# Moving side work inside a hand-ordered kernel: attention of two blocks, input parts of two blocks, the last weight pair

## The chip, the cores and the metric

The kernel runs on 1 core of one Trainium2 chip. The metric is device microseconds (us) of one execution, inputs and output in the chip's memory; lower is better. Three runs of the kernel before took 867.34, 867.5 and 868.3 us; their median is 867.5 us. The profile is one execution of its own.

## The reference

Everything is float32. Four batches of 576 positions and 8 heads of size 64 go through a linear attention, and the 2304 rows that come out through two feed-forward layers:

```
kv  = einsum('bhsd,bhse->bhde', k, v)
o   = einsum('bhsd,bhde->bhse', q, kv)
o   = o / sqrt(mean(o*o, axis=-1) + 1e-6) * g_norm     # to x: 2304 x 512
h   = x @ moe_w_in                                     # 512 x 2048
x1  = (h * sigmoid(h)) @ moe_w_out                     # 2048 x 512
out = ((x1 @ moe2_w_a) * (x1 @ moe2_w_b)) @ moe2_w_out # 512 x 1536 twice, 1536 x 512
```

## The kernel before

The 2304 rows are six blocks of 384, numbered 0 to 5. Activations lie transposed: a tile holds 128 features by 384 rows. Each float32 factor of a large product is split in two, a rounded high part (ACT copies it to the type fp32r) and the low rest (DVE subtracts); a product is high times high, low times high and high times low, three matmuls a term. The weights come as raw 128 x 512 pieces that ACT scales (L305, `dec_scale`) and DVE takes apart in three instructions (L311, L317, L324) before the split.

The program has these stretches, in the order of the span:

- 0 to 62 us: attention of blocks 0 and 1 and the first pieces of the first layer, by a list written out.
- 62 to 183 us: steps numbered `g` from 4 to 31. A step multiplies x of one block with one piece of `moe_w_in` (`hp`, L354), passes the result through ACT (sigmoid-weighted, then its high part `gh`, L364) and DVE (low part `gl`, L369), and multiplies the step before with `moe_w_out` (`x1p`, L380). Beside this, steps carry k^T v (`kvps`, L186), attention (`ao`, L220), its norm (`ss` L233, `rr` L238 on POOL, the multiplication L243) and the transposes to x (`xtp`, L256, which ACT copies out as `xf`, L915) of blocks 2 and 3. The `kvps`, `ao` and `xtp` tiles share two buffers of the matmul's output memory.
- to 277 us: eight units, 0 to 7, for blocks 2 and 3 together. A unit has seven products (`X_h`, `Z_h`, `Y_h`, `V_h`, L671) by a scheme with seven multiplications in the place of eight on sums of quarters; after each there is a hook, 0 to 6, into which other work is put. The h values go through DVE (`h`, L827) and ACT (`g`, L837). The sums of x that the scheme needs are the "x parts": pieces T1, hT1, hB11 and so on, in twelve small steps on ACT (L437) and DVE (L438, L487).
- to 335 us: steps on the second half of those units' h values, and beside them attention of blocks 4 and 5. Its q blocks (`qb`, L151) come in by DMA as 8 or 4 small transfers each, DVE transposes them (`qT`, L159), PE multiplies (`ao`).
- to 411 us: units 0 to 7 for blocks 4 and 5, and to 447 us steps again (`x1p`, with `gh_5_n` and `gl_5_n`).
- 447 us to the end: the second layer for blocks 0 and 1, 2 and 3, 4 and 5, from weight sums (`wd`) and x sums (`xcd`) that earlier stretches put into the chip's memory.

The weight sums of the second layer are made in pairs, n from 0 to 11 (`wa0`, `wb0`, `wa1`, ...). A pair is a load (two pieces) and six steps: scale both pieces on ACT; decode the first; decode the second and take the high part; sums (L545 to L548, into two tiles `s_0`, `s_1`); high parts; low parts. Steps hang on hooks of the units; those of the last pair, `wb10` and `wb11`, hang on steps of the stretch after 411 us.

The x sums of blocks 0 and 1 are made by `last_blocks` and `combine` for kt = 0 and kt = 1: `last_blocks` reads x1 of the two blocks back from memory (tiles `b_0_r` and `b_1_r`, four DMAs a kt, L1012), then twelve parts write sums and store them (`xcd`, L439), two small stores a part at most.

What sets the order: the whole program is written out by hand, and each engine works through its own list in order. All DMAs stand in one list, SP's, and are issued in order too: an issue that waits holds back all behind it. `put()` stands in the hooks of units 5 to 7 and releases the stores whose parts have been computed. Tiles are taken from pools. `page` has 37 buffers of 4 KB a partition and `six` has 6 larger ones; a buffer is handed on in the order in which it came free, and the first write into it waits for the last reader of the tile that had it before.

The lines that the change and the prediction touch: `at(g, f)` puts f into step g, `at_unit(b, u, n, f)` into hook n of unit u, `slot(b, h)` counts hooks through the units, seven a unit. `attend`, `turn_q`, `load_q_blocks`, `load_kv`, `kv_pair` are the attention pieces; each takes its step from a tuple of numbers. `prepare(kind, p, roomy)` makes a pair of weight sums; with `roomy` the tile `s_1` comes from `six`, else from `page`.

Of the kernel before, what the change touches and what calls it, by code (L numbers as in the profile page):

```python
# [60 lines left out]
def tile_linattn_moe_moe2(ctx: ExitStack, tc: tile.TileContext, q, k, v, g_norm,  # L61
# [31 lines left out]
    def page(shape, dt, name):  # L93
        return sb.tile(shape, dt, tag="page", bufs=NPAGE, name=name)
# [181 lines left out]
    def load_w(key):  # L276
        kind, f = key
        fs = slice(f * P, (f + 1) * P)
        src = srcs[kind]
        wide = src.dtype != F32  # L280
        if kind in ("wi", "wa", "wb"):
            src = src[:, fs]
        else:
            src = src[fs, :]
        if wide:
            src = src.bitcast(U32)
        if kind in ("wi", "wa", "wb"):
            src = src.rearrange("(kt p) f -> p kt f", p=P)
        r = page([P] + list(src.shape[1:]), U32 if wide else F32, f"raw_{kind}{f}")
        nc.sync.dma_start(r, src)  # L290
        raws[key] = r.rearrange("p k f -> p (k f)") if kind in ("wi", "wa", "wb") else r
# [4 lines left out]
    def dec_scale(key):  # L296
        r = raws[key]
        if r.dtype == F32:
            mids[key] = r
            return  # L300
        r = r.rearrange("p (n t) -> p n t", t=2)
        early = key[0] in ("wi", "wo") and key[1] < 4
        early = early or key[0] == "wb" and key[1] >= NF2 - 2
        m = (page if early else small)([P, DM], U32, f"m_{key[0]}{key[1]}")
        nc.scalar.mul(m.bitcast(F32), r[:, :, 1].bitcast(F32), 2.0 ** -112)  # L305
        mids[key] = m

    def dec_shift(key):
        m = mids[key]
        if m.dtype == U32:  # L310
            nc.vector.tensor_scalar(m, m, 3, None, op0=ALU.logical_shift_left)  # L311
# [15 lines left out]
    def dec_join(key):  # L327
        dec_low(key)
        dec_sign(key)
# [105 lines left out]
    def halve(hi, lo, src, *stores):  # L435

        return (lambda: nc.scalar.copy(hi, src),  # L437
                lambda: nc.vector.tensor_sub(lo, src, hi.bitcast(F32)),  # L438
                *[lambda to=to, t=t: nc.sync.dma_start(to, t.bitcast(F32)) for to, t in stores])  # L439
# [57 lines left out]
    def prepare(kind, p, roomy=False):  # L497


        keys = [(kind, 2 * p + f) for f in range(2)]  # L500
        mat = ("wa", "wb").index(kind)
        H2 = 2 * P
        m, s, wait = [], [], []

        def load():
            for key in keys:
                load_w(key)

        def decode(f):
            dec_shift(keys[f])  # L510
            dec_join(keys[f])
            m.append(mids.pop(keys[f]))

        def flat(t):
            return t.rearrange("p i f -> p (i f)")

        def hi(o, lo, src, to):
            first_, *rest = halve(o, lo, src, to)
            first_()
            wait.append(rest)  # L520

        def rest():
            sub, *put_ = wait.pop(0)
            sub()
            fresh_.extend(put_)

        def scale():
            dec_scale(keys[0])
            dec_scale(keys[1])

        def first_half():
            decode(0)

        def second_half():
            o = page([P, 2, DM], F32R, f"a_{kind}{p}")
            hi(o[:, 0], o[:, 1], m[0], (wd[p, (0, 4)[mat]], flat(o)))
            decode(1)

        def add():
            rest()  # L540
            for h in range(2):
                s.append((six if roomy and h else page)([P, 2, DM], F32R, f"s_{h}_{kind}{p}"))
            a11, a12, a21, a22 = (e[:, h * H2:(h + 1) * H2] for e in m for h in range(2))
            s1, s2, s3, s4 = (s[h][:, 1, i * H2:(i + 1) * H2].bitcast(F32) for h in range(2) for i in range(2))
            nc.vector.tensor_add(s1, a21, a22)  # L545
            nc.vector.tensor_sub(s3, a11, a21)
            nc.vector.tensor_sub(s2, s1, a11)
            nc.vector.tensor_sub(s4, a12, s2)  # L548

        def high():  # L550
            a21, a22 = m[1][:, 0:H2].bitcast(F32R), m[1][:, H2:]
            for h in range(2):
                o = s[h]
                hi(o[:, 0], o[:, 1], o[:, 1].bitcast(F32), (wd[p, ((1, 2), (5, 6))[mat][h]], flat(o)))
            hi(a21, a22.bitcast(F32R), a22, (wd[p, 3, :, mat * DM:(mat + 1) * DM], m[1].bitcast(F32R)))

        def low():
            for _ in range(3):
                rest()

        return load, [scale, first_half, second_half, add, high, low]
# [324 lines left out]
    base = []  # L886
    n = 0
# [5 lines left out]
    def at(g, fn, *args):  # L893
        side.setdefault(g, []).append(lambda: fn(*args))
# [27 lines left out]
    def at_unit(b, u, n, fn, *args):  # L922
        inner.setdefault((b, u, n), []).append(lambda: fn(*args))

    for b, g0s in ((2, (12, 14, 16, 18)), (3, (20, 22, 24, 26))):
        at(g0s[0] - 4, load_kvt, b)
        for g0, p in zip(g0s, (0, 2, 1, 3)):
            at(g0 - 3, load_kv, b, p)
            at(g0, kv_pair, b, p)
    for (j, p), g0 in zip([(2, 0), (2, 2), (3, 0), (3, 2), (2, 1), (2, 3), (3, 1), (3, 3)],  # L930
                          (12, 14, 16, 18, 20, 22, 24, 25)):
        at(g0 - 5, load_q_blocks, j, p)
        at(g0 - 2, turn_q, j, p)
        at(g0, attend, j, p)
        at(-(g0 + 1), norm_mul, j, p)
        at(g0 + 3, stage_f, j, p)
# [52 lines left out]
    def slot(b, h):  # L989
        return (b,) + divmod(min(h, 7 * NF1 // 2 - 1), 7)  # L990

    for n in range(2 * NPAIR):
        load, steps = prepare(("wa", "wb")[n % 2], n // 2, n <= 7)
        if n == 2 * NPAIR - 1:
            at_unit(4, 7, 3, load)
            for i, f in enumerate(steps):
                at(base[8] + 1 + i, f)
            continue
        b, h0 = (2, 7 * (n + 2)) if n < 3 else (4, 7 * (n - 3))
        if h0 == 0:  # L1000
            at(P2A + 14, load)
        else:
            at_unit(*slot(b, h0 - 5), load)
        for f, h in zip(steps, (0, 1, 2, 5, 5, 7)):
            at_unit(*slot(b, h0 + h), f)

    def last_blocks(d, kt):

        t = [page([P, 2, TB], F32, f"b_{kt}_{r}") for r in range(2)]
        for r in range(2):  # L1010
            for n in range(2):
                nc.sync.dma_start(t[r][:, n], x1d[2 * d + n, :, 2 * r + kt, :])  # L1012
        return lambda n, r: t[r][:, n]
# [6 lines left out]
    for kt in range(2):  # L1020
        todo = []

        def blocks0(kt=kt, todo=todo):
            todo.extend(combine(0, kt, half_page, last_blocks(0, kt)))

        def parts0(n, todo=todo):
            for f in todo[n]:
                f()

        at_unit(2, 5 + kt, 6, blocks0)  # L1030
        for n in range(12):
            at_unit(2, 6 + kt, 1 + n // 2, parts0, n)

    made = {}

# [175 lines left out]
    with tc.manual_schedule():  # L1211
# [64 lines left out]
        for n, (d, p) in enumerate(seq):  # L1276
            new = 0 < n < NPAIR
            m = n % NPAIR
            if 1 <= m <= 4 and n < 2 * NPAIR:

                kt, h = divmod(m - 1, 2)
# [53 lines left out]
```

## Time and profile before

| | |
|---|---|
| median of three runs | 867.5 us (867.34 to 868.3) |
| the profiled execution | 866.76 us, of which the span of the trace is 865.0 us |
| PE (TensorE matmul) busy | 850.8 us, 98% of the span, 4966 instructions |
| DVE (VectorE) busy | 622.2 us, 72% |
| ACT (ScalarE) busy | 347.8 us, 40% |
| POOL (GpSimd) busy | 52.6 us, 6% |
| DMA | 230 MB, all queues; 229.15 MB on SP's queue in 127904 packets |
| granted TensorE clock | the highest tenth in all 40 slices |

PE is busy in all but some 14 us, so the time is PE's work and its waits. The chain that ended last runs 83% on PE. Numbers in names are tile numbers of the program: `qb_5_3` is the q block of block 5 for the fourth pair of heads (pairs are numbered 0 to 3), `gl_5_2` the low part of step 2 of the stretch after unit 7. In the trace the numbers are left out.

### The profile page before, as it was taken

The page shows a single profiled execution, that of the slowest core. Times are in us where ns is not written, and L with a number is a line of the kernel's source. Part 1 is how long each engine was busy: PE and PEld are TensorE (multiplying, and loading weights), DVE is VectorE, ACT ScalarE, POOL GpSimd, SP SyncE. Part 2 cuts the span into 40 slices and gives each one's busy share as a digit, 9 for nine tenths or more (in the row PEclk, how much of TensorE's full clock was granted, in tenths as well). Part 3 has the DMA queues.
Part 4 walks back from the last instruction along what each step waited for, and adds up shares of the span by engine and source line. Part 5 has one row for each costly group of instructions (what it writes and reads, how often), then busy time and mean ns, then how long its engine had stood idle before and what let it go on. Part 6 is the DMA issues. An engine that isn't in the chain of part 4 may idle for free.

```text
span 865.0 us, 13734 instructions
## 1 busy us (share of the span) xinstructions
PE 850.8 (98%) x4966; PEld 807.4 (93%) x4967; DVE 622.2 (72%) x1191; ACT 347.8 (40%) x708; POOL 52.6 (6%) x73
## 2 busy tenths in 40 slices
PE   7999999999999999999999999999999999999998
PEld 5799999999998999999999999999999999999996
DVE  4879989777956779989746788876576665545555
ACT  4666765544545456556522533221412211221110
POOL 5430111100000500000000000000000000000000
PEclk9999999999999999999999999999999999999999
DMA  9985886189986659999999998496688475755001
GB/s 276 372 222 160 258 244 234 66 312 405 408 315 183 190 218 336 405 404 385 369 405 417 388 336 333 152 379 242 238 305 276 135 292 200 292 219 195 1 0 74
DMA packets 127972, 230.03 MB, mean 266 GB/s; under 512 B 41504, under 2 KB 87072, under 8 KB 127904
## 3 DMA queue, kind: packets, MB, share of 16 engines
q1 hardware_dynamic: 127904, 229.15, 73.7%
q8 instruction: 39, 0.64, 0.3%
q14 instruction: 29, 0.24, 0.1%
HBM read 160.17 MB, written 68.94 MB: 265 GB/s over the span
## 4 chain that ended last, share of the span: by engine, by line
PE 83%; DMA 9%; DVE 4%; ACT 2%; issue 1%; SPq 1%; POOL 0%; DVEq 0%; ACTq 0%
PE x1p L380 18%; PE op L865 17%; PE hp L354 8%; PE Z_b L671 4%; PE X_b L671 4%; PE V_b L671 4%; PE Z_a L671 4%; PE X_a L671 4%; PE V_a L671 4%; DMA wd<-a_wa 2%; PE V_h L671 2%; PE X_h L671 2%; PE Y_b L671 2%; PE Y_a L671 2%; PE Z_h L671 2%; PE ao L220 2%
## 5 line engine op out<-in xcount | busy, mean ns | idle before, releaser
L380 PE MATMUL x1p<-gh,wo 128*128 128x384 f32 x768 | 195.0, 337 | 0.3 <-ACT gh L364 0.3
L380 PEld LDWEIGHTS x1p<-gh,wo 128*128 128x128 f32 x768 | 138.0, 188 | 0.6 <-ACT gh L364 0.6
L380 PE MATMUL x1p<-gl,wo 128*128 128x384 f32 x384 | 127.9, 337 | 1.1 <-DVE gl L369 1.1
L865 PE MATMUL op<-wp,ab 128*128 128x512 f32 x360 | 83.4, 390 | 0.0
L728 ACT CAST ab<-a 128x384 fp32r<-128x384 f32 x72 | 37.0, 514 | 115.0 <-DVE a L722 58.3
L865 PEld LDWEIGHTS op<-wp,ab 128*128 128x128 f32 x360 | 67.4, 188 | 13.7
L369 DVE TENSOR_TENSOR gl<-g,gh 128x384 fp32r<-128x384 f32 x96 | 54.0, 563 | 30.6 <-ACT gh L364 30.4
L380 PEld LDWEIGHTS x1p<-gl,wo 128*128 128x128 f32 x384 | 71.9, 188 | 2.0 <-DVE gl L369 2.0
L873 DVE TENSOR_TENSOR o<-op,o 128x512 f32<-128x512 f32 x90 | 60.4, 686 | 16.6 <-PE op L865 16.6
L865 PE MATMUL op<-w,ab 128*128 128x512 f32 x288 | 66.9, 390 | 0.0
L865 PEld LDWEIGHTS op<-w,ab 128*128 128x128 f32 x288 | 53.9, 188 | 10.9
L364 ACT CAST gh<-g 128x384 fp32r<-128x384 f32 x96 | 49.2, 513 | 22.4 <-PE x1p L380 20.6
L354 PE MATMUL hp<-xh,wi 128*128 128x384 f32 x256 | 52.7, 345 | 0.4 <-ACT xh L260 0.3
L238 POOL TENSOR_TENSOR rr<-ss,nhalf 128x6 f32<-128x6 f32 x24 | 34.4, 1435 | 229.4 <-DVE ss L233 229.3
L354 PEld LDWEIGHTS hp<-xh,wi 128*128 128x128 f32 x256 | 43.8, 188 | 1.4 <-ACT xh L260 1.0
L671 PE MATMUL X_a<-xc,wp 128*128 128x384 f32 x216 | 43.8, 337 | 0.0
L671 PE MATMUL Z_a<-xc,wp 128*128 128x384 f32 x216 | 43.4, 335 | 0.1
L671 PE MATMUL V_a<-xc,wp 128*128 128x384 f32 x216 | 43.3, 335 | 0.0
L671 PE MATMUL Z_b<-xc,wp 128*128 128x384 f32 x216 | 43.3, 335 | 0.0
L671 PE MATMUL V_b<-xc,wp 128*128 128x384 f32 x216 | 43.3, 335 | 0.0
L671 PE MATMUL X_b<-xc,wp 128*128 128x384 f32 x216 | 43.3, 334 | 0.0
L732 DVE TENSOR_TENSOR ab<-a,ab 128x384 fp32r<-128x384 f32 x72 | 39.8, 553 | 2.2 <-ACT ab L728 0.6
(172 smaller groups left out, 1551.6 us busy)
## 6 DMA issues: line engine op xcount, KB each, us to landing
wp<-wd SPq DMA_DIRECT2D x114, 512.0 KB, 6.5
hw<-hsd SPq DMA_DIRECT2D x32, 512.0 KB, 8.5
xc<-xcd SPq DMA_DIRECT2D x21, 768.0 KB, 8.5
hw<-had SPq DMA_DIRECT2D x16, 768.0 KB, 8.4
raw_wi<-in_moe_w_in_dram SPq DMA_DIRECT2D x16, 512.0 KB, 7.0
raw_wo<-in_moe_w_out_dram SPq DMA_DIRECT2D x16, 512.0 KB, 6.0
hsd<-hs SPq DMA_DIRECT2D x16, 512.0 KB, 5.0
raw_wa<-in_moe_w_a_dram SPq DMA_DIRECT2D x12, 512.0 KB, 7.8
```

Source lines behind the costliest of these rows:

```text
L220: nc.tensor.matmul(o[a:e, i], t[:, i * P + a:i * P + e], kvc[bb, p], start=True, stop=True)
L238: nc.gpsimd.tensor_tensor(r, rms[j, p], nhalf, op=ALU.pow)
L354: nc.tensor.matmul(o, w[wp][:, kt * P:(kt + 1) * P], x[key][:, kt, :], start=(n == 0), stop=(n == 3 * KD - 1))
L364: nc.scalar.copy(gh, src)
L369: nc.vector.tensor_sub(gl, src, gh.bitcast(F32))
L380: nc.tensor.matmul(acc[vi][c], w[wp][:, c * P:(c + 1) * P], gg[vi, s][g], start=(s == s0 and i == 0), stop=(s == s1 - 1 and i == 2))
L671: nc.tensor.matmul(b[bank], w(name, wq, kt), x(i, xq, kt), start=(fresh and k == 0), stop=(k == 5), skip_group_check=True)
L728: nc.scalar.copy(o[:, 0], t)
L732: low = lambda t=t, o=o: nc.vector.tensor_sub(o[:, 1], t, o[:, 0].bitcast(F32))
L865: nc.tensor.matmul(o, ab[d, p, f, n][:, g, ts], wp[p, 7 + f][:, wq * DM:(wq + 1) * DM], start=(k == 0), stop=(k == 5))
L873: nc.vector.tensor_add(t, o, t)
```

## The change

Three edits.

1. k^T v of blocks 2 and 3 moves from steps 12, 14, 16, 18 and 20, 22, 24, 26 to 11, 13, 15, 17 and 19, 21, 23, 25; attention from 12, 14, 16, 18, 20, 22, 24, 25 to 11, 13, ... 25. Loads, q transposes, norms and `xtp` hang on these numbers and move along.
2. Of blocks 0 and 1, kt = 1: the four loads move from hook 6 of unit 6 to hook 3 of unit 6, and the twelve parts from hooks 1 to 6 of unit 7 to hooks 0 to 5. kt = 0 stays where it was.
3. The last pair of weight sums is loaded in hook 2 of unit 7 instead of hook 3, its six steps start in the first step of the stretch after 411 us instead of the second; and `prepare` is given room in `six` for pairs 0 to 6 instead of 0 to 7, so that `s_1_wb3` comes from `page`.

```diff
--- before.py
+++ after.py
@@ -922,13 +922,13 @@
     def at_unit(b, u, n, fn, *args):
         inner.setdefault((b, u, n), []).append(lambda: fn(*args))
 
-    for b, g0s in ((2, (12, 14, 16, 18)), (3, (20, 22, 24, 26))):
+    for b, g0s in ((2, (11, 13, 15, 17)), (3, (19, 21, 23, 25))):
         at(g0s[0] - 4, load_kvt, b)
         for g0, p in zip(g0s, (0, 2, 1, 3)):
             at(g0 - 3, load_kv, b, p)
             at(g0, kv_pair, b, p)
     for (j, p), g0 in zip([(2, 0), (2, 2), (3, 0), (3, 2), (2, 1), (2, 3), (3, 1), (3, 3)],
-                          (12, 14, 16, 18, 20, 22, 24, 25)):
+                          range(11, 27, 2)):
         at(g0 - 5, load_q_blocks, j, p)
         at(g0 - 2, turn_q, j, p)
         at(g0, attend, j, p)
@@ -990,11 +990,11 @@
         return (b,) + divmod(min(h, 7 * NF1 // 2 - 1), 7)
 
     for n in range(2 * NPAIR):
-        load, steps = prepare(("wa", "wb")[n % 2], n // 2, n <= 7)
+        load, steps = prepare(("wa", "wb")[n % 2], n // 2, n <= 6)
         if n == 2 * NPAIR - 1:
-            at_unit(4, 7, 3, load)
+            at_unit(4, 7, 2, load)
             for i, f in enumerate(steps):
-                at(base[8] + 1 + i, f)
+                at(base[8] + i, f)
             continue
         b, h0 = (2, 7 * (n + 2)) if n < 3 else (4, 7 * (n - 3))
         if h0 == 0:
@@ -1027,9 +1027,10 @@
             for f in todo[n]:
                 f()
 
-        at_unit(2, 5 + kt, 6, blocks0)
+        h0 = 43 + 6 * kt
+        at_unit(*slot(2, h0 - 2 - 2 * kt), blocks0)
         for n in range(12):
-            at_unit(2, 6 + kt, 1 + n // 2, parts0, n)
+            at_unit(*slot(2, h0 + n // 2), parts0, n)
 
     made = {}
```

SP's list, in units 6 and 7: `b_0_*` and `b_1_*` are the loads of x1 for kt = 0 and kt = 1, `xcd` the stores of x sums, first where the loads now stand.

```order
 L439 DMA xcd_71<-hB11_0_0_3070 128x384
 L439 DMA xcd_71<-b_0_0_3045 128x384
+L1012 DMA b_1_0_3118<-x1d_68 128x384 x2
+L1012 DMA b_1_1_3119<-x1d_68 128x384 x2
 L439 DMA xcd_71<-hT1_0_0_3073 128x384
 L439 DMA xcd_71<-hB11_0_0_3070 128x384
```

The second piece follows in the same list, six rows further on, where the loads stood; `qb_4_0` and those behind it are q blocks.

```order
 L439 DMA xcd_71<-hT2_0_0_3115 128x384
 L439 DMA xcd_71<-T2_0_0_3101 128x384
-L439 DMA xcd_71<-hB21_0_0_3163 128x384
+L439 DMA xcd_71<-hB21_0_0_3169 128x384
 L439 DMA xcd_71<-b_0_1_3046 128x384
-L1012 DMA b_1_0_3184<-x1d_68 128x384 x2
-L1012 DMA b_1_1_3185<-x1d_68 128x384 x2
-L439 DMA xcd_71<-hB21_0_0_3163 128x384
+L439 DMA xcd_71<-hB21_0_0_3169 128x384
 L439 DMA xcd_71<-hT2_0_0_3115 128x384
-L151 DMA qb_4_0_3209<-in_q_dram 32x6x32 x8
-L151 DMA qb_5_0_3218<-in_q_dram 32x12x32 x4
```

The four loads of `b_1_0` and `b_1_1` are moved ahead of ten stores; the first q load stood two stores behind them and now stands twelve behind. Rows taken out and put in with another number alone (`hB21_0_0`) are the same work; the q loads come again further down in their old order, with the stores of kt = 1 spread otherwise among them: before `qb_5_3`, the last q load, there were 44 q issues and 12 stores from `qb_4_0` on, and there are 44 and 14 now.

PE's list in step 25 (block 3, head pair 3), before:

```order
L380 MATMUL x1p_3_3_1736<-gh_3_12_1907,wo_12_1612 128x384 x2
L380 MATMUL x1p_3_3_1736<-gl_3_12_1912,wo_12_1612 128x384
L256 MATMUL xtp_2_3_1990<-ident_63,sq0_66 128x128 x3
L220 MATMUL ao_3_3_1995<-kvc_0_3_79,qT_3_3_1888 128x128 x3
L354 MATMUL hp_3_14_2009<-xh_1_531,wi_14_1803 128x384 x8
L354 MATMUL hp_3_14_2009<-xl_1_532,wi_14_1803 128x384 x4
```

And now:

```order
L380 MATMUL x1p_3_3_1745<-gh_3_12_1930,wo_12_1625 128x384 x2
L380 MATMUL x1p_3_3_1745<-gl_3_12_1935,wo_12_1625 128x384
L186 MATMUL kvps_3_3_1995<-kv_3_3_1836 64x64 x8
L186 MATMUL kvps_3_3_1995<-kvt_3_1384 64x64 x2
L220 MATMUL ao_3_3_2008<-kvc_0_3_79,qT_3_3_1911 128x128 x3
L354 MATMUL hp_3_14_2022<-xh_1_531,wi_14_1829 128x384 x8
L354 MATMUL hp_3_14_2022<-xl_1_532,wi_14_1829 128x384 x4
```

`ao_3_3` followed directly on `xtp_2_3`; now `xtp_2_3` stands a step ahead, and `kvps_3_3` has come between the step's `x1p` and `ao_3_3`.

DVE's list in the first steps after 411 us (`gl` is the low part that the next `x1p` needs; `m_wb10` and `m_wb11` are the last pair's pieces), before:

```order
L369 TENSOR_TENSOR gl_5_1_4988<-g1_4_0_3965,gh_5_1_4986 128x384
L369 TENSOR_TENSOR gl_5_2_5016<-g1_4_0_3965,gh_5_2_5014 128x384
L311 TENSOR_SCALAR m_wb10_5006<-m_wb10_5006 128x512
L317 SCALAR_TENSOR_TENSOR m_wb10_5006<-raw_wb10_4878,m_wb10_5006 128x512
L324 SCALAR_TENSOR_TENSOR m_wb10_5006<-raw_wb10_4878,m_wb10_5006 128x512
L369 TENSOR_TENSOR gl_5_3_5043<-g1_4_0_3965,gh_5_3_5041 128x384
L311 TENSOR_SCALAR m_wb11_5008<-m_wb11_5008 128x512
L317 SCALAR_TENSOR_TENSOR m_wb11_5008<-raw_wb11_4880,m_wb11_5008 128x512
L324 SCALAR_TENSOR_TENSOR m_wb11_5008<-raw_wb11_4880,m_wb11_5008 128x512
L369 TENSOR_TENSOR gl_5_4_5068<-g1_4_1_4226,gh_5_4_5066 128x384
```

And now:

```order
L369 TENSOR_TENSOR gl_5_1_4992<-g1_4_0_3965,gh_5_1_4990 128x384
L311 TENSOR_SCALAR m_wb10_4980<-m_wb10_4980 128x512
L317 SCALAR_TENSOR_TENSOR m_wb10_4980<-raw_wb10_4868,m_wb10_4980 128x512
L324 SCALAR_TENSOR_TENSOR m_wb10_4980<-raw_wb10_4868,m_wb10_4980 128x512
L369 TENSOR_TENSOR gl_5_2_5019<-g1_4_0_3965,gh_5_2_5017 128x384
L311 TENSOR_SCALAR m_wb11_4982<-m_wb11_4982 128x512
L317 SCALAR_TENSOR_TENSOR m_wb11_4982<-raw_wb11_4870,m_wb11_4982 128x512
L324 SCALAR_TENSOR_TENSOR m_wb11_4982<-raw_wb11_4870,m_wb11_4982 128x512
L369 TENSOR_TENSOR gl_5_3_5048<-g1_4_0_3965,gh_5_3_5046 128x384
L438 TENSOR_TENSOR a_wb5_5033<-m_wb10_4980,a_wb5_5033 128x512
```

The decoding of each piece stands one `gl` sooner; on ACT the scaling of both pieces stood behind `gh_5_1` and now stands ahead of it.

## Rows read from the trace of the kernel before

**Rows 1.** The page: busy time of each engine, its share, and instructions.

```profile
PE 850.8 (98%) x4966; PEld 807.4 (93%) x4967; DVE 622.2 (72%) x1191; ACT 347.8 (40%) x708; POOL 52.6 (6%) x73
```

**Rows 2.** Timeline of PE (start, duration, engine, line, tile, [idle before <-releaser]): five waits.

```profile
155.74 0.94 PE L220 MATMUL ao<-kvc,qT 128*128 128x128 f32 x6 [0.67 <-ACT xf L915]
...
272.49 1.34 PE L671 MATMUL Z_h<-hB_h,hw 128*128 128x384 f32 x6 [0.23 <-DVE h L827]
...
277.40 0.44 PE L380 MATMUL x1p<-gl,wo 128*128 128x384 f32 x1 [1.15 <-DVE gl L369]
...
395.13 1.31 PE L671 MATMUL V_h<-hT_h,hw 128*128 128x384 f32 x6 [0.70 <-DVE u_h L681]
...
425.86 0.62 PE L380 MATMUL x1p<-gh,wo 128*128 128x384 f32 x2 [0.26 <-ACT gh L364]
```

**Rows 3.** Timeline of the DMA queue SP from 256 to 298 us: issues.

```profile
256.33 0.32 SPq L439 DMA_DIRECT2D xcd<-b  x1
...
256.74 0.38 SPq L439 DMA_DIRECT2D xcd<-hT  x1
...
263.46 0.38 SPq L439 DMA_DIRECT2D xcd<-b  x1
...
263.93 1.87 SPq L1012 DMA_DIRECT2D b<-x1d  x4
...
266.84 12.21 SPq L151 DMA_DIRECT2D qb<-in_q_dram  x24
...
296.05 2.01 SPq L151 DMA_DIRECT2D qb<-in_q_dram  x4
```

**Rows 4.** Timeline of PE: unit 6's Z, unit 7's Y, an xtp of block 5.

```profile
260.45 1.21 PE L671 MATMUL Z_h<-hB_h,hw 128*128 128x384 f32 x6
...
262.54 1.21 PE L671 MATMUL Y_h<-hT_h,hw 128*128 128x384 f32 x6
...
301.64 0.49 PE L256 MATMUL xtp<-ident,sq 128*128 128x128 f32 x3
```

**Rows 5.** Timeline of DVE from 269 to 301 us.

```profile
269.81 0.56 DVE L487 TENSOR_TENSOR b<-b,b 128x384 f32<-128x384 f32 x1 [1.02 <-DMA b<-x1d]
...
276.80 0.55 DVE L369 TENSOR_TENSOR gl<-g,gh 128x384 fp32r<-128x384 f32 x1
...
300.04 0.58 DVE L159 STREAM_TRANSPOSE qT<-qb 128x384 f32<-128x384 f32 x1 [0.68 <-DMA qb<-in_q_dram]
...
300.54 0.52 DVE L243 TENSOR_TENSOR sq<-ao,rr 128x384 f32<-128x384 f32 x1
```

**Rows 6.** Timeline of DVE and PE from 90 to 94 us.

```profile
90.04 0.55 DVE L369 TENSOR_TENSOR gl<-g,gh 128x384 fp32r<-128x384 f32 x1
...
93.46 0.57 DVE L159 STREAM_TRANSPOSE qT<-qb 128x384 f32<-128x384 f32 x1
...
91.49 0.34 PE L380 MATMUL x1p<-gl,wo 128*128 128x384 f32 x1
```

**Rows 7.** Timeline of ACT from 415 to 425 us.

```profile
415.62 0.52 ACT L364 CAST gh<-g 128x384 fp32r<-128x384 f32 x1
...
416.03 1.23 ACT L305 ACTIVATE m_wb<-raw_wb 128x512 f32<-128x512 f32 x2
...
424.75 0.66 ACT L584 ACTIVATE m_w<-raw_w 128x512 f32<-128x512 f32 x1 [2.87 <-DMA raw_w<-in_moe_w_out_dram]
```

**Rows 8.** Timeline of DVE and PE from 417 to 420 us.

```profile
418.17 0.42 DVE L311 TENSOR_SCALAR m_wb<-m_wb 128x512 uint32<-128x512 uint32 x1
...
419.95 0.55 DVE L369 TENSOR_TENSOR gl<-g,gh 128x384 fp32r<-128x384 f32 x1
...
417.47 0.34 PE L380 MATMUL x1p<-gl,wo 128*128 128x384 f32 x1
```

**Rows 9.** Timeline of DVE: decoding of the w_a pair before 390 us.

```profile
387.19 0.43 DVE L545 TENSOR_TENSOR s_wa<-m_wa 128x256 f32<-128x256 f32 x1 [0.79 <-DMA wd<-a_wb]
...
388.66 0.43 DVE L546 TENSOR_TENSOR s_wa<-m_wa,m_wa 128x256 f32<-128x256 f32 x1 [1.05 <-DMA wd<-s_wb]
```

## The prediction

> **What bounds the kernel now.** I read the page first. PE is busy 850.8 us, 98% of the span [rows 1], so no engine has to be made faster. The change adds and removes no instruction of PE, DVE, ACT or POOL, and can only take away waits of PE or make new ones. Then I looked through PE's timeline for idle time in the stretches that the edits touch. Five waits lie there [rows 2]: 0.67 us before an `ao` at 155.74 (the `ao` of block 3, pair 3, whose output buffer was that of an `xtp` that ACT had still to copy), 0.23 and 1.15 us in unit 7 (`Z_h` at 272.49, `x1p` at 277.40, both held by DVE), 0.70 us at 395.13, 0.26 us at 425.86. Their sum, 3.01 us, is all that the edits could win there. Third came the issues of SP, the DMA queue, around unit 7 [rows 3], and DVE beside them [rows 5]: here the reader is to see that SP issues one small DMA after another without a pause, and that the last q transpose already waits for it.
>
> **Edit 1, attention.** `ao_3_3` no longer follows directly on `xtp_2_3`, a step of matmuls lies between them, so the copy by ACT (xf) is long done: minus 0.67 [rows 2]. The other `kvps`, `ao` and `xtp` stand to each other as before, a step earlier. What is late next is DVE, which has no free time in steps 10 to 13: a q transpose (0.57 us busy [rows 6]) and a norm's sum come ahead of `gl` where they came behind it. The `gl` at 90.04 ended at 90.59 and its matmul came at 91.49 [rows 6], a slack of 0.90; the two inserted instructions cost half a us each, 1.0 together, and the step's matmuls themselves come a little earlier by what k^T v weighs there. I take plus 0.2 for this step and the one before. The bounds are minus 0.67 with no new wait, and plus 0.5 if such a wait comes in two steps. Edit 1: minus 0.5. The loads that move with it still land more than a step before their use; that cover gone, a wait on one q block would cost the 0.5 us that a late issue costs.
>
> **Edit 2, the x parts.** What it can win is clear: in unit 7 DVE stands 1.02 us for the kt = 1 load at 269.81, and the `gl` at 276.80, which ends at 277.35, starts behind the parts that this held up [rows 5]; PE's 0.23 and 1.15 go, 1.38 us, when the parts come a hook sooner.
>
> What it costs stands on SP. The loads now precede ten stores, and they cannot be issued at once, because their tiles take over buffers still in use: `b_1_0` that of `hw_2_6_2`, which the last matmul of unit 6's `Z_h` reads, and `b_1_1` that of `hT2_h2_0`, which unit 7's `Y_h` reads up to its fifth of six matmuls (the pools' order of release gives both). In the trace these end at 260.45 + 1.21 = 261.66 and at about 262.54 + 0.9 = 263.4 [rows 4]; all of it comes 0.5 earlier by edit 1, so 262.9 for the second. Before, SP used just this time for the ten stores: 256.74 to 263.46 [rows 3]. Now it waits, in order, with the stores behind.
>
> Step by step: the last two loads take 2 x 0.47 (four took 1.87 [rows 3]), up to 263.85. Twelve stores follow, at the pitch of the queue: 24 q issues took 12.21 us, 0.51 each [rows 3], so 12 x 0.51 = 6.1, up to 269.95. There the q loads begin; before they began at 266.84 [rows 3], so they are 3.1 late. From there to the first issue of `qb_5_3` at 296.05 there were 29.2 us for 56 issues, no slack to catch up, and there are now 58. At 0.51 to 0.52 each that ends at 299.6 to 300.2, 3.6 to 4.1 late. I take 3.7.
>
> The transpose of `qb_5_3` waited 0.68 for its DMA, at 300.04 [rows 5], so it has no slack, and comes at 303.74. Next in DVE's list is the norm's multiplication (300.54 [rows 5]), on which PE's `xtp` at 301.64 depends [rows 4]: it ended at 301.06, 0.5 before PE came to it with everything else done. So `xtp` starts at 301.64 + 3.7 - 0.5 = 304.84. This is a point in time, not a delay to be added to others: PE would arrive there at 301.64 - 0.5 - 1.38 = 299.76 and waits, in one piece or with the q blocks before it sharing it. The gains of edits 1 and 2 vanish in it. Balance at 301.64: plus 3.2. The bounds: minus 1.9 if SP is not late, plus 4.5 if each issue behind the loads takes the 0.52 us and `b_1_1` is issued a little later still.
>
> The trace says of issuing that it is slow: 0.51 us each, 24 on end [rows 3]. The Trainium skill (DMA: Bandwidth & Descriptors, section Issuing engines are not separate DMA queues) says that the time to initiate a DMA is usually small beside the DMA itself. By that rule 12 stores ahead of the q loads would cost next to nothing and edit 2 would win its 1.38. The measured pitch decides against it for such small transfers; what it would give is the first rival below.
>
> **Edit 3, the last weight pair.** On ACT the two scalings (1.23 us as a group, some 1.1 up to the next start, since instructions overlap a little [rows 7]) now come ahead of `gh_5_1`, which started at 415.62: it ends at 417.25 and `gl_5_1` at 417.85. PE's first matmul with `gl_5_1` stood at 417.47 [rows 8], so PE waits 0.4. Then each decoding, 418.17 to 419.95 = 1.78 us of DVE [rows 8], stands ahead of a `gl` whose step is only four groups of 0.52 = 2.08 us long. Followed through with these durations, the next four steps wait 0.15, 0.2, 0.45 and 0.3 more: 1.5. Before, the stretch lost 0.26 at 425.86 and the `gl` behind it, some 0.7 in all, because ACT stood 2.87 for a DMA at 424.75 [rows 2, 7]; that wait is now inside the others. Edit 3 net: plus 0.7, bounds 0 and plus 1.3.
>
> `s_1_wb3` from the other pool shifts every later `page` buffer by one. The next pair's `s_0_wa4` then waits for the store of `s_0_wb3`, a later one than before; already now DVE waits 0.79 and 1.05 for such stores [rows 9], and `V_h` at 395.13 is 0.70 late [rows 2] by DVE. This may get worse or better by that 0.7; I take plus 0.1.
>
> **Sum.** Plus 3.2 at 301.64, plus 0.7, plus 0.1: 4.0 us. Against the profiled execution, 866.76 us, that is 870.8. The median of the runs, 867.5, lies 0.74 above it, so a timed run should give 871.5.
>
> **The rivals.**
>
> *SP catches up.* The loads find their buffers free earlier than I read it, or the stores are issued faster than 0.51. Then minus 0.67 and minus 1.38 stand, with edit 3 between 0 and 0.8: 865.4 to 866.3. For it: the pitch in the middle of stores has been 0.47, and b loads and stores need no new data. Against it: 56 issues in 29.2 us leave nothing to give back. It decides when the q loads start before 267.5. 12 in 100.
>
> *The q loads are half as late.* With 2 us of lateness `xtp` is at 303.1, plus 1.5 at 301.64, and with the rest of edit 3 low the sum is 0 to plus 2.3: 867.5 to 869.8. It would come if some stores wait no longer behind the loads, or q blocks land quicker than the 2 us that they took. 22 in 100, half of it within the measurement.
>
> *Only PE's list counts.* Lateness is hidden since DVE's list leaves other work to PE; edits 1 and 3 nearly cancel, and 1.38 is lost again elsewhere: no change, 866.5 to 868. The wait of 0.68 already there [rows 5] speaks against it. 10 in 100.
>
> *It is worse.* The same lateness, and DVE in steps 10 to 13 or at 395 loses another 2 us: 873.5. 6 in 100.
>
> **How the numbers follow.** My forecast, 871.5 with an own range of 870 to 873, has 50 in 100. What can be told from no change for this kernel is about 0.2%, 1.7 us: slower means above 869.2, faster below 865.8. Slower: 50 + 6 + 11 of the half-late case = 67. Within: 11 of the half-late case, 10 of no change and 2 of the first rival = 23. Faster: the first rival's other 10. The range that holds 8 in 10 goes from 866.3, which leaves the first rival out, to 873.2.
>
> **What the new profile would show.** Right: SP's list pauses before the b loads at 261 to 263, q loads start near 270, the last q transpose of block 5 waits some 3 us for its DMA, and PE has a wait of 1 to 4 us before an `xtp` near 300 to 305, while the waits at 155.74 and 277.40 are gone. After 415 us, PE shows small waits on `gl` in four or five steps on end. Wrong: if the q loads start by 267, or PE runs from 285 to 307 without a wait on `xtp`, the main step has failed; if the first `gl` after 415 us is in time, that of edit 3.

## The result, and the profile after

The changed kernel took 871.73 us, the median of 6 runs (870.72 to 873.57), against 867.8 us of before in 6 runs: ratio 1.0052, 95% interval 1.0034 to 1.0069. It is slower by 3.9 us between the medians, by 4.5 going by the ratio. The profiled execution is one of the slower of these, 873.32 us with a span of 871.5; before it was 866.76. What the two traces show is therefore 6.6 us of difference, not 3.9; the part that only some runs have is the last point of this section.

PE's instructions are the same in number, and their busy time rose all the same, from 850.8 [rows 1] to:

```profile
PE 854.4 (98%) x4966; PEld 808.7 (93%) x4967; DVE 620.7 (71%) x1191; ACT 348.1 (40%) x708; POOL 52.7 (6%) x73
```

Of PE's timeline the waits between 150 and 435 us, which answer to [rows 2]:

```profile
257.23 1.32 PE L671 MATMUL V_h<-hT_h,hw 128*128 128x384 f32 x6 [0.65 <-DVE u_h L681]
...
269.41 1.32 PE L671 MATMUL V_h<-hT_h,hw 128*128 128x384 f32 x6 [0.42 <-DVE u_h L681]
...
284.43 0.55 PE L256 MATMUL xtp<-ident,sq 128*128 128x128 f32 x3 [0.52 <-DVE sq L243]
...
291.40 0.55 PE L256 MATMUL xtp<-ident,sq 128*128 128x128 f32 x3 [0.20 <-DVE sq L243]
...
299.41 0.55 PE L256 MATMUL xtp<-ident,sq 128*128 128x128 f32 x3 [1.24 <-DVE sq L243]
...
305.74 0.90 PE L256 MATMUL xtp<-ident,sq 128*128 128x128 f32 x3 [2.65 <-DVE sq L243]
...
389.54 1.34 PE L671 MATMUL V_h<-hT_h,hw 128*128 128x384 f32 x6 [0.98 <-DVE u_h L681]
...
431.14 0.44 PE L380 MATMUL x1p<-gl,wo 128*128 128x384 f32 x1 [0.18 <-DVE gl L369]
```

Of the five waits of before none is left at its place; a `V_h` one unit ahead of that of 395.13 waits 0.98, at 389.54, and a `gl` at 431.14 0.18. New are four waits for an `xtp`, 0.52 + 0.20 + 1.24 + 2.65 = 4.6 us, all released by DVE's norm multiplication. The last one stood at 301.64 [rows 4] and stands at 305.74.

SP's list from 256 to 303 us, which answers to [rows 3] (four loads of x1, then stores, then the q loads):

```profile
256.74 0.32 SPq L439 DMA_DIRECT2D xcd<-b  x1
261.72 2.71 SPq L1012 DMA_DIRECT2D b<-x1d  x4
264.52 0.38 SPq L439 DMA_DIRECT2D xcd<-hT  x1
...
270.53 0.41 SPq L439 DMA_DIRECT2D xcd<-hT  x1
271.00 5.93 SPq L151 DMA_DIRECT2D qb<-in_q_dram  x12
...
277.96 12.93 SPq L151 DMA_DIRECT2D qb<-in_q_dram  x24
...
292.91 3.87 SPq L151 DMA_DIRECT2D qb<-in_q_dram  x8
296.88 0.39 SPq L439 DMA_DIRECT2D xcd<-T  x1
...
300.84 2.01 SPq L151 DMA_DIRECT2D qb<-in_q_dram  x4
```

The reader is to see the hole between 257.06 and 261.72, and then no hole any more: what SP did not do in it comes behind it. The waits of SP in this stretch name the cause, the two matmul groups that still read the buffers (columns: us in total, times, longest):

```profile
SPq L1012 <- PE Z_h L671: 4.6, 1, 4.6
...
SPq L1012 <- PE Y_h L671: 0.8, 1, 0.8
```

The q loads begin at 271.00 (before 266.84), the last begins at 300.84 (before 296.05). DVE's q transposes, which answer to the third of [rows 5], now wait for nearly every q block; the four of those waits that stand ahead of the four `xtp` waits, and the multiplication behind the last:

```profile
283.35 0.58 DVE L159 STREAM_TRANSPOSE qT<-qb 128x384 f32<-128x384 f32 x1 [2.66 <-DMA qb<-in_q_dram]
...
290.32 0.58 DVE L159 STREAM_TRANSPOSE qT<-qb 128x384 f32<-128x384 f32 x1 [2.32 <-DMA qb<-in_q_dram]
...
298.34 0.58 DVE L159 STREAM_TRANSPOSE qT<-qb 128x384 f32<-128x384 f32 x1 [3.36 <-DMA qb<-in_q_dram]
...
304.66 0.58 DVE L159 STREAM_TRANSPOSE qT<-qb 128x384 f32<-128x384 f32 x1 [2.96 <-DMA qb<-in_q_dram]
305.16 0.52 DVE L243 TENSOR_TENSOR sq<-ao,rr 128x384 f32<-128x384 f32 x1
```

The last point is PE's clock. The windows of the changed kernel around the last wait (columns: PE, PEld, DVE, ACT, POOL busy with instructions, granted clock, DMA share, GB/s):

```profile
302.00:305.00 3.00, 1.09 (x7) 0.77 (x5) 0.34 (x1) 1.39 (x4) 0.00 (x0) 1.00 0.79 222
305.00:307.00 2.00, 1.26 (x6) 1.27 (x7) 2.00 (x5) 0.32 (x1) 0.78 (x1) 0.63 0.96 249
307.00:309.00 2.00, 2.00 (x10) 2.00 (x9) 1.51 (x4) 1.25 (x4) 0.85 (x2) 0.52 1.01 378
309.00:311.00 2.00, 2.00 (x14) 1.97 (x13) 2.00 (x6) 0.43 (x2) 1.56 (x1) 1.00 1.01 405
```

PE was idle for 2.65 of the 3 us before 305.74, and then got a clock of 0.63 and 0.52 of full speed in two windows, where the kernel before has 1.00; full speed is the level of 2.4 GHz, a half that of 1.2 GHz. Some 3.4 us at half speed, by the clock of these windows, cost this execution 1.5 to 1.7 us (the same matmuls start 4.1 us behind those of before at 305.74 and 5.6 to 5.8 us behind some 10 us later). Of the six runs four have a mean clock of 0.997 or 0.998 and took 871.2 to 873.57; the two with 1.000 took 870.72 and 870.77. Of the 60 runs of the kernel before beside the experiments one has a mean clock as low as 0.998.

### The profile page after: what moved, and what is told of

Read it like the earlier page. It is cut to its first block, busy times and chain, and to the rows that moved or that the text cites. A ratio compares the mean times of both kernels' runs of the same rounds, so it can differ in the third digit from the quotient of the medians.

```text
span 871.5 us, 13730 instructions
## 1 busy us (share of the span) xinstructions
PE 854.4 (98%) x4966; PEld 808.7 (93%) x4967; DVE 620.7 (71%) x1191; ACT 348.1 (40%) x708; POOL 52.7 (6%) x73
## 4 chain that ended last, share of the span: by engine, by line
PE 80%; DMA 8%; DVE 6%; SPq 3%; issue 2%; ACT 1%; POOL 0%; DVEq 0%; ACTq 0%
PE x1p L380 16%; PE op L865 16%; PE hp L354 8%; PE X_b L671 4%; PE Z_a L671 4%; PE V_b L671 4%; PE X_a L671 4%; PE Z_b L671 4%; PE V_a L671 4%; DMA wd<-s_wa 4%; PE V_h L671 2%; PE X_h L671 2%; PE Z_h L671 2%; SPq L151 2%; PE Y_b L671 2%; PE Y_a L671 2%
```

## The experiments

The theory: SP's list is what costs. The moved loads wait on SP for buffers in use, the twelve stores behind them are put off, and so are the q loads, up to the last, on which PE waits by way of DVE. The rival: the time goes elsewhere, by the parts a hook sooner, by edit 1 or by edit 3. Each kernel ran with kernels of before on the same chip; ratios are to before, and a time against before is the ratio's. A time against the changed kernel is taken from the medians, 871.73 us there; by the ratios it comes out up to 0.4 us larger.

**Each edit alone.** Edit 1 (steps 11, 13, ... in place of 12, 14, ...):

```diff
-    for b, g0s in ((2, (12, 14, 16, 18)), (3, (20, 22, 24, 26))):
+    for b, g0s in ((2, (11, 13, 15, 17)), (3, (19, 21, 23, 25))):
-                          (12, 14, 16, 18, 20, 22, 24, 25)):
+                          range(11, 27, 2)):
```

> The kernel before with edit 1 alone. My theory (the changed kernel loses its time on SP's list, by edit 2): the 0.67 us wait before ao goes, and the trace of the changed kernel stood 1.0 us ahead of before at 190 us; so 0.5 to 1.0 us faster than before, ratio 0.9988 to 0.9994, and the waits at 272 and 277 us stay. Rival (the new places of attention load DVE or SP in the steps and cost later): 1 us or more slower than before.

Measured: 865.99 us, ratio 0.9989 (0.9980 to 0.9998), faster by 0.95. No wait of PE is left at 155. In unit 7 the wait at 277 is still there, and in place of 0.23 before `Z_h` there is one of 0.55 before `V_h`:

```profile
268.80 1.33 PE L671 MATMUL V_h<-hT_h,hw 128*128 128x384 f32 x6 [0.55 <-DVE u_h L681]
...
276.82 0.44 PE L380 MATMUL x1p<-gl,wo 128*128 128x384 f32 x1 [1.12 <-DVE gl L369]
```

So the theory's first term holds and the rival falls. Matmul for matmul, PE gains 0.75 us on the kernel before between 30 and 170 us of this trace.

Edit 2 (loads three hooks sooner, parts one hook sooner):

```diff
-        at_unit(2, 5 + kt, 6, blocks0)
+        h0 = 43 + 6 * kt
+        at_unit(*slot(2, h0 - 2 - 2 * kt), blocks0)
-            at_unit(2, 6 + kt, 1 + n // 2, parts0, n)
+            at_unit(*slot(2, h0 + n // 2), parts0, n)
```

> The kernel before with edit 2 alone. My theory: SP stands still for some 4 us ahead of the kt = 1 loads, the q loads start near 271 us, xtp waits some 4 us in all between 284 and 307; 3 to 5 us slower than before, with a dip of PE's granted clock between 300 and 310 us. Rival (the three edits cost only together, or edit 3 costs most): within 1.5 us of before.

Measured: 873.3 us, ratio 1.0063 (1.0050 to 1.0076), slower by 5.5; a little more than the theory's 5, and far from the rival's 1.5. Its trace has the same waits as the changed kernel:

```profile
298.64 0.55 PE L256 MATMUL xtp<-ident,sq 128*128 128x128 f32 x3 [1.28 <-DVE sq L243]
...
305.08 0.86 PE L256 MATMUL xtp<-ident,sq 128*128 128x128 f32 x3 [2.75 <-DVE sq L243]
```

and four of its five runs show a mean clock of 0.998 or less. The last `xtp` stands at 305.08 without edit 1 and at 305.74 in the changed kernel with it, so what edit 1 wins is lost in this wait.

Edit 3 (last pair a step sooner, one tile from the other pool):

```diff
-        load, steps = prepare(("wa", "wb")[n % 2], n // 2, n <= 7)
+        load, steps = prepare(("wa", "wb")[n % 2], n // 2, n <= 6)
-            at_unit(4, 7, 3, load)
+            at_unit(4, 7, 2, load)
-                at(base[8] + 1 + i, f)
+                at(base[8] + i, f)
```

> The kernel before with edit 3 alone. My theory: small waits on gl after 415 us and a shift of the V_h wait at 395; 0.3 to 1.3 us slower than before, ratio 1.0003 to 1.0015. Rival (edit 3 carries a good part of the loss): over 2 us slower. Second rival (edit 3 costs nothing): within 0.3 us.

Measured: 867.54 us, ratio 1.0003 (0.9994 to 1.0012): plus 0.3 us, not to be told from nothing nor from the lower part of what was expected. Over 2 us is out. The `V_h` wait has shifted as expected (0.65 at 384.82, before 0.70 at 395.13 [rows 2]), and of the waits on `gl` the trace names one, 0.18 at 426.29. Its profiled execution shows something of the kernel before, in a stretch that edit 3 does not touch: a group of 20 q issues took 12.11 us where it had taken 10.62, and PE waited for the last `xtp`. In the kernel before:

```profile
280.37 10.62 SPq L151 DMA_DIRECT2D qb<-in_q_dram  x20
```

With edit 3:

```profile
280.45 12.11 SPq L151 DMA_DIRECT2D qb<-in_q_dram  x20
...
297.62 2.00 SPq L151 DMA_DIRECT2D qb<-in_q_dram  x4
```

```profile
302.67 0.55 PE L256 MATMUL xtp<-ident,sq 128*128 128x128 f32 x3 [1.57 <-DVE sq L243]
```

The last q load came 1.57 us later than at 296.05 [rows 3], and `xtp` 1.03 later than at 301.64 [rows 4]; PE's wait is longer than that because PE came 0.5 earlier. Where the last `xtp` waits, in this trace and in those of the changed kernel, of edit 2 and of the POOL version below, it starts 4.9 to 5.1 us behind the first issue of the last q load; in the kernel before it started 5.6 behind it. So the kernel before stands near the edge itself: it has some 0.5 us to spare, as the prediction had it, and any delay on SP beyond that reaches PE one to one. With edits 1 and 2 PE would come 2 us earlier to a q load that is 4 to 5 us later.

**The wait moved off SP.** In the changed kernel the four loads are issued by POOL at the same place:

```diff
-                nc.sync.dma_start(t[r][:, n], x1d[2 * d + n, :, 2 * r + kt, :])
+                q = nc.gpsimd if (d, kt) == (0, 1) else nc.sync
+                q.dma_start(t[r][:, n], x1d[2 * d + n, :, 2 * r + kt, :])
```

> The changed kernel, with the four kt = 1 loads of blocks 0 and 1 issued by POOL instead of SP at the same place of the program. The wait for the buffers then holds POOL, which has nothing to do there, and SP goes on with the stores. My theory (the loss is SP standing still): q loads start before 267 us, xtp waits 1.5 us at most in all, PE's clock does not dip; 866.5 to 868.5 us, 3 to 5 us faster than the changed kernel. Rival (the loss comes from the parts a hook sooner, which move 14 stores ahead of the last q load, or from the number of DMAs): less than 1.5 us faster than the changed kernel.

Measured: 866.15 us, ratio 0.9985 (0.9976 to 0.9994), 5.6 us faster than the changed kernel, somewhat more than expected: the loss comes by SP's list, and the rival falls. POOL now issues the loads when the buffers come free, and SP is at the q loads at 263.80, 7.2 us earlier than in the changed kernel's trace:

```profile
259.68 2.35 POOL L1013 DMA_DIRECT2D b<-x1d  x4 [100.80 <-DMA xcd<-hT]
```

```profile
263.80 8.00 SPq L151 DMA_DIRECT2D qb<-in_q_dram  x12
...
295.87 2.01 SPq L151 DMA_DIRECT2D qb<-in_q_dram  x4
```

```profile
269.39 1.33 PE L671 MATMUL V_h<-hT_h,hw 128*128 128x384 f32 x6 [1.70 <-DVE u_h L681]
...
301.00 0.55 PE L256 MATMUL xtp<-ident,sq 128*128 128x128 f32 x3 [0.59 <-DVE sq L243]
```

Counted from the store `xcd<-b` ahead of the moved loads (255.00 in this trace), SP needs 8.8 us to the q loads; in the changed kernel it needed 14.3 (from 256.74), before 10.5 (from 256.33 [rows 3]). So the standing still is worth some 3.7 us, and another 1.7 are the four issues that SP no longer makes; this run takes both off and does not show them apart.

What is left: 0.59 us at the last `xtp`, as expected, and a wait that I had not expected, 1.70 us for `V_h` at 269.39. DVE stands there ahead of the first kt = 1 part, with the `u_h` that PE needs behind it:

```profile
266.03 0.56 DVE L487 TENSOR_TENSOR hB<-b 128x384 f32<-128x384 f32 x1 [2.67 <-issue]
```

The profile names no releaser here. That it is the data of the loads, which POOL has issued up to 262.03, so that the parts a hook sooner come before their data, is argued and not shown by this trace; the next one names them.

**The loads put back, the parts left a hook sooner.**

```diff
-        at_unit(*slot(2, h0 - 2 - 2 * kt), blocks0)
+        at_unit(*slot(2, 41 + 7 * kt), blocks0)
```

> The changed kernel with the four kt = 1 loads put back to hook 6 of unit 6, behind the ten stores; the twelve parts stay a hook sooner, edits 1 and 3 stay. My theory (the place of the loads on SP's list costs the time): q loads start near 266.5 us in place of 271, the waits on xtp fall from 4.6 us to 2.5 or less, no dip of the clock; 867 to 869 us, 2.5 to 5 us faster than the changed kernel. Rival (the parts a hook sooner are what costs): at most 1 us faster than the changed kernel.

Measured: 867.75 us, ratio 1.0003 (0.9990 to 1.0016), 4.0 us faster than the changed kernel. The time is as expected and the way there is not. The profiled execution is the longest of the twelve, 869.86 us; in it no `xtp` waits at all, because PE loses its lead before, in one piece, at unit 7's `V_h`, and the clock falls, which I had not expected (seven of the twelve runs have a mean clock of 0.998 or less):

```profile
271.18 2.29 PE L671 MATMUL V_h<-hT_h,hw 128*128 128x384 f32 x6 [3.11 <-DVE u_h L681]
```

```profile
268.00:271.00 3.00, 0.07 (x1) 0.00 (x0) 2.27 (x5) 1.15 (x3) 0.00 (x0) 0.93 0.78 219
271.00:274.00 3.00, 2.82 (x9) 2.82 (x10) 3.00 (x8) 1.96 (x6) 0.00 (x0) 0.50 0.48 78
274.00:277.00 3.00, 3.00 (x11) 3.00 (x10) 1.89 (x4) 1.36 (x4) 0.00 (x0) 0.50 0.58 168
277.00:280.00 3.00, 3.00 (x17) 3.00 (x17) 1.50 (x3) 1.04 (x2) 0.00 (x0) 0.93 0.39 64
```

DVE waits 3.23 us for the loads in the part moved to hook 0:

```profile
267.21 0.56 DVE L487 TENSOR_TENSOR hB<-b 128x384 f32<-128x384 f32 x1 [3.23 <-DMA b<-x1d]
```

So the parts a hook sooner are a cost by themselves when the loads are not there; the rival has a share here that the changed kernel does not show, since there its loads land earlier.

**Fewer stores ahead of the last q load.** In the changed kernel the stores computed from hook 4 of unit 7 on are released behind the last q load, eight of them:

```diff
-        for n in range(7):
+        for n in range(7 if u < 7 else 4):
             at_unit(2, u, n, lambda: put())
```

> The changed kernel, loads where it has them, but the stores of kt = 1 that stand between the last two q loads (eight of them) are released behind the last q load. My theory (each small DMA ahead of the last q load puts it off by 0.51 us, and PE with it): the last q load is issued 4.1 us earlier, near 296.8; the wait of 2.65 us at the last xtp goes, and with it the dip of the clock; the waits before it (1.2, 0.5, 0.2) stay; 867 to 869 us. Rival (the q loads are late because they start late, and the stores between them do not matter): 871 us or more.

Measured: 867.5 us, ratio 0.9999 (0.9987 to 1.0011), 4.2 us faster than the changed kernel. The last q load comes directly behind the one before it, the last `xtp` no longer waits, the clock stays at 1.00 in the window from 300 to 310 us, and the waits before it have stayed:

```profile
291.16 5.88 SPq L151 DMA_DIRECT2D qb<-in_q_dram  x12
```

```profile
282.86 0.55 PE L256 MATMUL xtp<-ident,sq 128*128 128x128 f32 x3 [0.63 <-DVE sq L243]
...
297.68 0.55 PE L256 MATMUL xtp<-ident,sq 128*128 128x128 f32 x3 [1.29 <-DVE sq L243]
```

SP still stands still and starts its q loads late here (269.18), so a late start alone does not cost the 4.2 us, and the rival falls. Nor do the eight stores alone: the kernel before had ten in their place (291.09 to 295.54 of its trace). The lateness of the last q load is a sum, and either part taken off, SP's standing still or the eight stores, gives back most of the loss; what the change itself added to it is the standing still and two stores. The time is at the low end of the expected range: the 2.65 and the clock's part behind it are gone together.

**A version that beats both.** Edit 1, the loads three hooks sooner and by POOL (diff above), the parts where they were, no edit 3:

```diff
-        at_unit(2, 5 + kt, 6, blocks0)
+        at_unit(*slot(2, 41 + 4 * kt), blocks0)
```

> The kernel before with edit 1, and with the four kt = 1 loads three hooks sooner but issued by POOL; the parts stay at their old hooks, edit 3 is left out. My theory: the loads are there before the parts, SP has four issues fewer ahead of the q loads, so the waits at 269 and 277 us of edit 1 alone (0.55 and 1.12) go and no xtp waits; 1.0 to 2.0 us faster than edit 1 alone, 864 to 865.2 us. Rival (POOL issues too late, or the wait only moves): as edit 1 alone, 866 us.

Measured: 864.77 us, ratio 0.9972 (0.9960 to 0.9985). Of unit 7's waits 0.17 us at 274.80 is left, no `xtp` waits. Against edit 1 alone that is 1.5 us by the ratios, as expected, though the two intervals overlap; the trace shows where it comes from, the waits of 0.55 and 1.12. The last `xtp` starts 4.9 us behind the last q load: it does not wait, and has nothing to spare.

With the stores behind the q loads as well (diff above):

> As the kernel with edit 1 and the loads by POOL, and with the stores of kt = 1 behind the last q load as well. My theory: the q loads have slack of some 5 us, so a late issue on SP no longer reaches PE; as that kernel or up to 0.5 us faster, with a narrower spread of the runs; 863.5 to 865.2 us. Rival (the stores behind the q loads put off the weight loads of the next units): 1 us or more slower than it.

Measured: 864.08 us, ratio 0.9964 (0.9949 to 0.9978), 3.1 us faster than before and 7.6 faster than the changed kernel. Against the version without it the intervals overlap, so the stores' part is not settled, while the rival's loss of 1 us is not seen; the runs' spread did not become narrower (862.67 to 867.12), as I had expected it to. PE's waits from 265 to 310 us in its trace:

```profile
274.73 0.44 PE L380 MATMUL x1p<-gl,wo 128*128 128x384 f32 x1 [0.56 <-DVE gl L369]
```

## Why the prediction was right, and where it was not

The time (871.5 against 871.73), the sign and the mechanism came out. By its steps:

- *Edit 1, minus 0.5.* The 0.67 went, and the `gl` of steps 10 to 13 made no new wait: none of 0.15 us or more is left on PE between 62 and 183 us in the new trace. The 0.2 set aside for them was not needed; alone the edit gave 0.95, with an interval that holds 0.2 to 1.7, and 0.75 in its trace.
- *Edit 2, the gain of 1.38.* Both waits are gone, and two on `V_h` (0.65 and 0.42, in units 6 and 7) stand in their place, which I had not in the sum. DVE was not ready with `u_h`: in unit 6 it had stood in a part of kt = 0 for its load, in unit 7 for ACT, with the parts ahead of `u_h` in its list. It had no weight in the end, as the gain was lost at `xtp` anyway. DVE's two waits:

```profile
255.50 0.56 DVE L487 TENSOR_TENSOR hB<-b 128x384 f32<-128x384 f32 x1 [3.48 <-DMA b<-x1d]
...
264.36 0.56 DVE L438 TENSOR_TENSOR b<-b,hB 128x384 fp32r<-128x384 f32 x1 [2.31 <-ACT hB L437]
```

- *Edit 2, the lateness.* Loads issued up to 263.85: 264.43. Q loads from 269.95: 271.00. Last q load 3.6 to 4.1 late: 4.8. The pitch was right (58 issues from 271.00 to 300.84 are 0.514 each); what was short by 0.6 was the wait for the buffers, because PE was hardly earlier in unit 7 than before (`Y_h` at 262.56, before 262.54 [rows 4]; I had set 0.5), and 0.4 in the stores, one of which took 0.79. PE had lost its lead in the 0.65 at unit 6's `V_h`, which belongs to this execution: the kernel with fewer stores is the same program up to there, has no such wait, and its q loads begin at 269.18. The prediction's first paragraph has SP issuing without a pause; that holds from 263.46 on, while the ten stores ahead of it had pauses of up to 1.27 us. Balance at the last `xtp`: plus 3.2 forecast, plus 4.1 measured.
- *The clock was not in the sum.* It costs 1.5 to 1.7 us in the profiled execution, some 3.4 us at half clock. I had a wait of several us on PE in the forecast and priced it at its length alone. This is the term that was missing.
- *Edit 3, plus 0.7 and plus 0.1.* It was 0.3 alone, and its interval holds anything from minus 0.5 to plus 1.0. (The 1.5 less 0.7 of the prediction is 0.8; it took 0.7.) In the new trace the same matmuls start 6.2 us behind those of before at 407 us of before's time, 7.5 behind at 424 and 6.9 behind from 437 on: the `gl` are late, by 1.3 us where 1.5 was forecast, and half of that is given back where ACT had waited for a DMA before [rows 7]. Of the small waits on `gl` that were to show, the profile names one, 0.18 at 431.14; the others are too short for it. The rest, 0.3 to 0.7 us between 411 and 447 us in the five traces with edit 3, lies below what the timed runs of edit 3 alone can tell.

So 871.5 was hit in part by chance. The two runs without the dip of the clock, at 870.7, are 2.9 us above before, 1.1 less than the 4.0 of a sum that has no clock in it; the four with it, 872.6 in the mean, are 4.8 above. The median lies between. That the two ran without the dip is read from their mean clock alone, and where their 1.1 us went is open, since no trace is of such a run. The step that carried the sign, SP's wait and the q loads behind it, is what the POOL version and the one with fewer stores showed.

The Trainium skill (DMA: Bandwidth & Descriptors, section Issuing engines are not separate DMA queues) says that the time to initiate a DMA is usually small beside the DMA itself. For each DMA alone the trace of the kernel before agrees: some 0.5 us to issue, against a median from issue to landing of 2.0 us for q loads of 24 KB, 4.1 for those of 48 KB and 3.2 to 4.0 for the stores. What the prediction drew from it for its first rival, that twelve stores on one list would then cost next to nothing, does not follow and did not hold: the issues add up, and 8 stores, some 4 us of issuing, decide over 4.2 us of the changed kernel. The same section says that initiating DMAs on several engines only saves the sequencer's time for it. The POOL version saved that for four issues, 1.7 us, and besides it the time in which SP stood still.

## What to carry to other kernels

A transfer that is put earlier on a queue that issues in order must be able to go at once: look up what reads its buffer, and when, before counting the gain; if it has to wait, let an idle engine issue it. Count small DMAs ahead of a load with no slack: each puts it off by its issue time, 0.5 us here, and adds to any standing still ahead of them. The lateness comes to one point in time that swallows what was won before it. PE's waits of 2.65 us and more cost more than their length here, as the clock fell with them.

## What was not expected of the hardware

After an idle time of 2.65 us (of 2.75 and 3.11 in two experiments) PE ran for some 3.4 us, and 6.8 behind the longest, at half of its clock, while after waits of 1.2 to 1.7 us it stayed at 1.00. In the experiment with the loads put back the two windows from 271 to 277 us have a clock of 0.50, and 3 us passed with 9 and 11 matmul instructions where the window from 277 has 17.
